# Two more chunks of an attention are turned by strided copies and VectorE, in a kernel that feeds a mixture of experts

## The chip, the cores and the metric

The kernel runs on one core of a Trainium2 chip. The engines of that core are PE (TensorE, the matrix array, with its weight loads shown apart as PEld), DVE (VectorE), ACT (ScalarE), POOL (GpSimd) and SP (SyncE, which here does nothing but issue transfers); 16 DMA engines move the data. Each engine works through its own queue in order, and semaphores tie the queues together. The metric is the device time of one execution in microseconds (us); a kernel's time is the median over its runs.

## The reference

Everything is float32. A lightning attention with a decay per head runs over 4 batches, 8 heads, 768 positions and 64 columns a head, in blocks of 64 positions. Its output, turned to 3072 rows of 512, goes through four experts (512 to 1024 to 512) whose results are added with normalised weights.

```python
for b in range(nb):                       # blocks of 64 positions
    intra = (qb @ kb^T * Dmask) @ vb      # Dmask: lam ** distance, lower triangle
    inter = (qb * lam_pow) @ kv_state
    out[:, :, sl] = intra + inter
    kv_state = lam_block * kv_state + (kb * rev_pow)^T @ vb
x = out.transpose(0, 2, 1, 3).reshape(3072, 512)
for e in range(4):
    h = maximum(x @ w1[e], 0)
    y += p[:, e:e + 1] * (h @ w2[e])      # p: domain_probs, each row divided by its sum
```

## The kernel before

**Tiling.** The 3072 rows are 24 chunks of 128 positions (n = 0 to 23: two blocks of one batch, all heads), in three groups g of eight. `where(n)` gives a chunk's place along the sequence and its batch: chunks 8 to 11 are the third and fourth 128 positions of batches 0 and 1, chunk 12 the third of batch 2. The expert products of a group with an expert are a unit; there are twelve, and each runs as fast-multiplication products M1 to M7 (seven products in place of eight, on sums and differences of blocks, and the same again inside each), in the order M1, M5, M6, M2, M7, M3, M4 (`SEQ`).

**The main loop.** For each unit (`at`) and each of its seven products (`i`) there are eight steps (`x`), numbered (at·7 + i)·8 + x through the whole kernel. In the stretch that matters here a step is eight matmuls of PE, by turns of the second product of one unit (`second_product`, L1233, x even) and of the first product of the next unit (`first_product`, L1174, x odd); at x = 5 there are four. So unit number 2 of the first products runs while `at` is 1 (steps 56 to 111), and unit 3 while `at` is 2 (from 112). Step 73 is the first that multiplies by M6's weight operand of unit 2, step 129 that of unit 3. Each step also takes a job or two from lists for VectorE (`lately`, `background`, `own_sums`), feeds a weight operand (`feed`), lets the attention work due at this step go, issues a small copy (`trickle`) at some steps, and pumps the planner.

**Weight operands.** The operands of the first products are sums of blocks of w1. GpSimd makes them (`prepare_w1`): in a row M1, the sum S1, M5, S3, M7, S2 (with a load of a block), M6, M2, S4, M3, M4. Each M is four subtractions into a stage tile `ops`, which is stored to a scratch tensor in DRAM (`w_ops` in the profile); each S is two additions or subtractions into a stage tile `w1o`. `feed` on SP reads an operand back from DRAM into two tiles `ws_in`, part a (384 KB) and part b (512 KB), nine or so steps before PE reads them. The stage tiles are a ring of seven buffers, shared by the loaded blocks (`w1b`), `w1o`, `ops` and the tiles `to` below, so a new one waits until the tile that had its buffer is stored.

These jobs are called chores. The planner that puts them in the queues while the program is built keeps estimates of what each engine has been given. In `pump` (L208) a chore begins only if GpSimd is free by its estimate and the transfers asked for (`asked`, `moved`) are less than `FULL` = 4 steps ahead. If `feed` needs an operand that has not been made, `until` (L232) forces chores to begin there and then.

**The attention.** A group's chunks run among the products of the group before. For each chunk a run stands at a step of the hand-written list `AT` (chunk 8 at 34, 9 at 40, and so on): `both` first finishes the chunk before (`values`, L824 and L842, tiles `op`), then starts its own (`scores`, L761 and L768, tiles `sp`). The chunk's q and k must be turned first, so that the columns of the heads lie on the partitions. There are two ways. Through PE: `turn` (L714) makes eight transposes (L727, into the banks `qp` and `kp`) and two copies on ACT (L735, L736), four steps before the run. Or across, from chunk `FIRST_ACROSS` on: pieces of q and k are copied from DRAM to DRAM (tile `across`) so that each 32 columns of a head stand as rows of 128 bytes (`bring_across`, `trickle`); `load_across` loads the chunk as `qx` and `kx`, 12 steps before the run, and VectorE turns their blocks of 32 by 32 (`turn_across`, L707), seven steps before it. The pieces of a batch are issued in the order of `rank`; `load_more` first issues all pieces that its batch still needs. A piece holds all the positions of the batch from the first chunk that comes across.

The output of two chunks is gathered in two tiles `xc`. Then `pair_sums` (L874), a chore too, stores them to `x_blocks`, makes four differences on GpSimd (tile `to`), and stores these.

Of the kernel before, what the change touches and what calls it, by code (L numbers as in the profile page):

```python
# [21 lines left out]
def kernel(  # L22
# [40 lines left out]
    CPG = 8  # L63
# [4 lines left out]
    W = 512  # L68
# [54 lines left out]
    def vector(n, psum):  # L123
        filled[0] = max(filled[0], now[0] + psum / 2) + 0.09 + n * (0.31 if psum else 0.8 if spare else 0.49) / 512
# [357 lines left out]

    FIRST_ACROSS = CPG + 4
    across = dram.tile([2, P, NHP, B, 16, 32], FP32, name="across")
    pieces = []
    rank = {0: 0, 2: 1, 3: 2, 1: 3}

    def bring_across(b):  # L490
        c = min(where(n)[0] for n in range(FIRST_ACROSS, NG * CPG) if where(n)[1] == b)
        for x, of in enumerate((q, k)):
# [8 lines left out]
    def trickle(m=1, by=None):  # L501
        for _ in range(m):
            if pieces:
                pieces.pop(0)[1](by)

    def comes_across(n):
        return n >= FIRST_ACROSS

# [133 lines left out]
    background = []  # L642
# [15 lines left out]
    def fits():  # L658
        return filled[0] - now[0] < 0.6
# [42 lines left out]
    def turn_across(n):  # L702

        qT, kT = nat.pop((n, "qx")), nat.pop((n, "kx"))

        def across(x):
            nc.vector.transpose(out=x[:], in_=x[:])  # L707
            vector(W, False)
            if x is kT:
                turned[n] = qT, kT, qT  # L710

        soon(n, *(lambda x=x: across(x) for x in (qT, kT)))
# [172 lines left out]
        ))  # L885

    FILL = {1: 18, 2: 43}
    AT = (34, 40, 47, 53, 58, 91, 99, 108, 115, 147, 154, 167, 172, 203, 210, 223)
    V_AHEAD = {CPG + 10: 8, CPG + 13: 10}
    steps = []  # L890

    def attention():

        first, last = CPG, NG * CPG - 1
        for n in range(first, last + 1):
            s = AT[n - first]
            turns_at = s - (7 if comes_across(n) else 4)
# [952 lines left out]
    for at, (g, e) in enumerate(units):  # L1850
        if at == 0:
            chores.extend(prepare_w2(2) + prepare_w1(3) + prepare_w2(3))
            chores.extend(prepare_w2_ops(2, False) + prepare_w1(0))
            for x in (3, 0):
                chores.extend(prepare_w2_ops(x, True))
        ahead = units[at + 1] if at + 1 < len(units) else None
        nested, nests = at >= NEST, ahead and at + 1 >= NEST
        if at == NEST:
            until(("w1", 0, "M4"))
            chores.extend(prepare_w2_ops(1, True))  # L1860
            spare.append(True)
        if at == NEST - 1:
            packed.append(True)
        blocks, banks = {}, {}
        for i in range(7):
            if fill2:
                feed2(*fill2.pop(0))
            if not nested:
                later_operands(g, e, SEQ2[i])
            if nested or (nests and i == 6):  # L1870
                for _ in range(4 if not nested else 2 if ahead else 16 if i == 0 else 4 if i > 1 else 0):
                    if fill3:
                        feed3(*fill3.pop(0))
            if nests and i == 2:
                nc.scalar.dma_start(
                    out=gate_bc, in_=gate_rows[ahead[0] - 1, :, ahead[1]].partition_broadcast(P),
                )
            if nested:
                pair = (at * 7 + i) % 2 if ahead else i % 3
                idle[:] = [(("q11", "q12"), ("q01", "q02"))[pair % 2], False]  # L1880
                b = nested_product(at, SEQ3[i], (("q01", "q02"), ("q11", "q12"), ("g1", "g3"))[pair])
                if i < 6 and (at, SEQ3[i + 1]) != PLAIN:
                    inner_sums(at, SEQ3[i + 1])
            else:
                b = second_product(g, e, SEQ2[i], banks)
            if nests and i == 6:
                inner_sums(at + 1, SEQ3[0], nested)
                if at + 1 == EARLY[0]:
                    inner_sums(*EARLY, True)
            a = []  # L1890
            if ahead:
                a = first_product(*ahead, SEQ[i], blocks, ("g1", "g3"))
            if nested and (at, SEQ3[i]) == END:
                b[6:6] = [lambda: (give("M4", 1, ("s0", "s1"), (1,)), turn_end(1, "q11"))]
                b[5:5] = [lambda: (give("M4", 0, ("s0", "s1"), (1,)), turn_end(0, "q12"))]
            if not ahead:
                order = [[], b[0:2], [], b[2:4], [], b[4:6], [], b[6:]]
            elif nested:
                order = [b[0:2], a[0:2], b[2:4], a[2:4], b[4:5], a[4:6], b[5:8], a[6:]]
            else:  # L1900
                order = [b[0:1], a[0:2], b[1:2], a[2:4], b[2:3], a[4:6], b[3:5], a[6:]]
            turned_back = list(after_last.get(SEQ3[i], ())) if nested and not ahead else []
            if at == i == 0:
                for m in SEQ[1:]:
                    own_x_apart(m, g, 0)
            resting[0] = at == NEST - 1 and i >= 5 or at == NEST and i == 0 or at == NEST - 2 and i == 5
            for x, part in enumerate(order):
                for f in part:
                    if f:
                        f()  # L1910
                now[0] += 1
                put = False
                if at == 0:
                    idle[:] = [("s0", "s1"), i < 3]
                    put = put_back()
                    take(own_sums)
                if nested and ahead:
                    idle[1] = x in ((1, 4) if i < 5 or at > NEST + 1 else (4,)) and (at - 2 * E + 1, i, x) not in held_at
                    put = put_back()
                added = first_steps.pop((at - 2 * E + 1, i, x), None)  # L1920
                if added:
                    added()
                all_added(now[0])
                if joins and not background:
                    joined()
                elif added and x > 2 or put:
                    pass
                elif (ahead or x % 2 == 0 and x + i) and not (nests and i == 6 and x == 7):
                    if nested or nests:
                        if lately:  # L1930
                            take(lately)
                        else:
                            rest()
                        if at == 2 * E and i in (2, 3) and fits():
                            rest()
                    else:
                        took = False
                        for of in (lately, background, own_sums):
                            if of and (not took or fits() or of is background and len(of) > 4):
                                take(of)  # L1940
                                if of is lately and i == 0:
                                    take(of)
                                took = True
                if nested or nests:
                    take(aside)
                    if own_sums and (nested or fits()):
                        take(own_sums)
                if ending and fits():
                    end_first()
                if nested and ahead and x in (1, 3) and fill3:  # L1950
                    feed3(*fill3.pop(0))
                if turned_back and x > 0:
                    for y in turned_back.pop(0):
                        if SEQ3[i] == END[1]:
                            give(*y[:2], ("s0", "s1"), *y[2:])
                        else:
                            give_across(*y)
                if fill and at * 7 + i >= 6 and x in ((0, 1) if at * 7 + i < 13 else (1, 3, 5) if at * 7 + i == 13 else FEED[nested]):
                    feed(*fill.pop(0))
                while steps and (at * 7 + i) * 8 + x == steps[0][0]:  # L1960
                    steps.pop(0)[1]()
                if at == 0 or x % 2 or at == 1 and x == 4:
                    trickle(1, nc.scalar if x % 2 else None)
                for h in range(1, NG):
                    if x == 3 and 0 <= at * 7 + i - FILL[h] < 7:
                        x_fill(h, SEQ[at * 7 + i - FILL[h]])
                pump(PACE[g])
# [30 lines left out]
```

## Time and profile before

| | |
|---|---|
| median of three runs | 1141.27 us (1141.19 to 1144.36) |
| profiled execution | 1142.07 us, its span 1140.3 us |
| PE busy | 99% of the span |
| DVE, POOL, ACT busy | 67%, 67%, 33% |
| transfers | 267.12 MB in 326,828 packets, 153,216 of them under 512 B |
| chunk copies `across` | 128 pieces, on the queues of SP and of ACT |
| loads of `qx`, `kx` from `across` | 12 each, 256 KB, 4.8 us to landing (median) |

The profile is of one execution, whose own time is 1142.07 us; the span, from the first to the last recorded instruction, is 1.8 us shorter. Times of PE, DVE, ACT and POOL are busy times; a queue such as SPq shows issuing, and a transfer lands some microseconds after its issue. A row of the timeline gives start, duration, engine, line, operation, tiles and count; in brackets stand the idle time before it and what ended it. Nearly all operations of DVE and POOL are issued by a helper at L117 and nearly all transfers by one at L114, so the tiles tell them apart.

### The profile page before, as it was taken

What the parts mean: (1) busy time and instruction counts of PE and PEld (TensorE: products, weight loads), DVE (VectorE), ACT (ScalarE), POOL (GpSimd) and SP (SyncE); (2) the same over time, 40 slices, a digit from 0 to 9 for tenths busy, and PEclk for the clock granted to TensorE, in tenths of its full rate; (3) what the DMA queues carried; (4) which work ended last, traced back from release to release, by engine and by line L of the source; (5) the groups of instructions that cost most, each with busy time, mean ns of one, the idle gap of its engine ahead of it and who ended that gap; (6) DMA issues with size and microseconds to landing.
All of it is one profiled execution on the core that took longest, in us unless ns stands there. A gap on an engine that the chain in (4) does not pass through costs nothing.

```text
span 1140.3 us, 22080 instructions
## 1 busy us (share of the span) xinstructions
PE 1130.5 (99%) x7983; PEld 988.2 (87%) x7983; DVE 769.0 (67%) x1474; ACT 380.3 (33%) x768; POOL 761.0 (67%) x730
## 2 busy tenths in 40 slices
PE   8999999999999999999999999999999999999998
PEld 7888888888888888888888888888888888888887
DVE  4576776587577658737655566878767576776785
ACT  3325123212312321232343442444354452342332
POOL 2838147644843786447687997994996873873885
PEclk9999999999999999999999999999999999999999
DMA  9795889999899989769557858886577757657552
GB/s 204 180 287 166 212 222 279 291 270 335 262 292 320 316 291 282 222 222 314 177 177 261 283 180 281 290 272 204 180 264 244 218 162 207 194 160 211 171 194 74
DMA packets 326828, 267.12 MB, mean 234 GB/s; under 512 B 153216, under 2 KB 270144, under 8 KB 326720
## 3 DMA queue, kind: packets, MB, share of 16 engines
q1 hardware_dynamic: 289472, 258.14, 73.1%
q10 hardware_dynamic: 37216, 7.57, 3.5%
q8 instruction: 64, 1.05, 0.4%
q14 instruction: 44, 0.36, 0.1%
q0 software_dynamic: 32, 0.00, 0.0%
HBM read 197.97 MB, written 73.96 MB: 238 GB/s over the span
## 4 chain that ended last, share of the span: by engine, by line
PE 98%; DVE 1%; issue 0%; DMA 0%; ACT 0%; DVEq 0%; POOLq 0%; ACTq 0%
PE pg L1174 41%; PE pq L1550 25%; PE q L1233 21%; PE pM L1692 2%; PE pc L1692 2%; PE op L824 1%; PE sp L761 1%; PE op L842 1%; PE sp L768 1%; PE pM L1417 1%; PE pg L1550 1%; PE qp L727 1%; PE kp L727 0%; DMA decay<-in_lam_dram 0%; PE yp L1377 0%
## 5 line engine op out<-in xcount | busy, mean ns | idle before, releaser
L1174 PE MATMUL pg<-xs,ws_in 128*128 128x256 f32 x1960 | 470.1, 380 | 0.0
L1174 PEld LDWEIGHTS pg<-xs,ws_in 128*128 128x128 f32 x1960 | 371.1, 190 | 52.8 <-DVE m L117 2.4
L117 DVE TENSOR_TENSOR m<-pg,m 128x512 f32<-128x512 f32 x374 | 255.4, 685 | 92.4 <-PE pg L1174 82.5
L1233 PE MATMUL q<-w2t,m 128*128 128x256 f32 x1120 | 265.6, 380 | 0.0
L1233 PEld LDWEIGHTS q<-w2t,m 128*128 128x128 f32 x1120 | 211.7, 190 | 29.3 <-issue 0.3
L117 DVE TENSOR_TENSOR sums<-pq,sums 128x256 f32<-128x256 f32 x272 | 112.9, 420 | 90.6 <-PE pq L1550 76.9
L1550 PE MATMUL pq<-acc,w2t 128*128 128x256 f32 x688 | 169.2, 379 | 0.0
L117 POOL TENSOR_TENSOR m<-m,decay 128x512 f32<-128x512 f32 x91 | 114.5, 1270 | 78.7 <-ACT m L1191 52.1
L1550 PEld LDWEIGHTS pq<-acc,w2t 128*128 128x128 f32 x688 | 130.6, 190 | 17.9
L1191 ACT ACTIVATE m<-m 128x512 f32<-128x512 f32 x99 | 62.4, 630 | 192.5 <-DVE m L117 190.6
L1251 DVE SCALAR_TENSOR_TENSOR acc<-q,gate,acc 128x256 f32<-128x256 f32 x108 | 52.0, 482 | 79.1 <-PE q L1233 78.6
L117 DVE TENSOR_TENSOR m<-m,m 128x512 f32<-128x512 f32 x108 | 92.9, 861 | 6.5 <-ACT m L1157 6.5
L1187 ACT COPY m<-pg 128x512 f32<-128x512 f32 x88 | 51.5, 585 | 122.0 <-PE pg L1174 108.7
L1151 ACT COPY pg<-m 128x512 f32<-128x512 f32 x77 | 45.4, 590 | 113.0 <-DVE m L117 103.3
L117 POOL TENSOR_TENSOR acc<-hT,hT 128x512 f32<-128x512 f32 x56 | 70.3, 1272 | 15.0 <-PE pq L1550 9.9
L117 POOL TENSOR_TENSOR acc<-hT,acc 128x512 f32<-128x512 f32 x56 | 71.2, 1272 | 6.4 <-PE pq L1550 2.7
L1550 PE MATMUL pq<-hT,w2t 128*128 128x256 f32 x288 | 70.0, 379 | 0.0
L117 POOL TENSOR_TENSOR w2o<-w2b 128x512 f32<-128x512 f32 x26 | 33.9, 1325 | 45.8 <-DMA w2b<-in_moe_w_dram 39.3
L1550 PEld LDWEIGHTS pq<-hT,w2t 128*128 128x128 f32 x288 | 54.7, 190 | 7.4
L1155 ACT COPY m<-pg 128x512 f32<-128x512 f32 x44 | 25.7, 585 | 89.6 <-PE pg L1174 84.8
L1550 PE MATMUL pq<-m,w2t 128*128 128x256 f32 x228 | 55.4, 379 | 0.0
L1005 ACT COPY hp<-m 128x512 f32<-128x512 f32 x84 | 48.5, 589 | 15.6 <-DVE hT L117 14.1
(157 smaller groups left out, 1419.5 us busy)
## 6 DMA issues: line engine op xcount, KB each, us to landing
ws_in<-w_ops SPq DMA_DIRECT2D x40, 512.0 KB, 5.1
w2t<-w_ops SPq DMA_DIRECT2D x72, 256.0 KB, 3.2
ws_in<-w_ops SPq DMA_DIRECT2D x60, 256.0 KB, 3.5
ws_in<-w_ops SPq DMA_DIRECT2D x40, 384.0 KB, 4.0
w2b<-in_moe_w_dram SPq DMA_DIRECT2D x56, 256.0 KB, 5.0
w_ops<-ops SPq DMA_DIRECT2D x28, 512.0 KB, 5.5
w_ops<-ops SPq DMA_DIRECT2D x54, 256.0 KB, 4.3
w2t<-w_ops SPq DMA_DIRECT2D x100, 128.0 KB, 2.8
```

Source lines behind the costliest of these rows:

```text
L117: eng.tensor_tensor(out=o, in0=a, in1=b, op=op)
L727: nc.tensor.transpose(out=x[:, ac * C:(ac + 1) * C], in_=y[:, ac].rearrange("p r d -> p (r d)"), identity=ident[:],)
L1005: nc.scalar.copy(out=there[x][:], in_=blk[at][:])
L1151: nc.scalar.copy(out=banks[tags[1]][:], in_=new["11"][:])
L1155: nc.scalar.copy(out=o[:], in_=p[:])
L1174: nc.tensor.matmul(out=p[:, j * 256:(j + 1) * 256], lhsT=ws[i][:, j * P:(j + 1) * P], rhs=xs[i], start=(fresh and j == 0), stop=True, skip ...
L1187: nc.scalar.copy(out=new[at][:], in_=p[:])
L1191: nc.scalar.activation(out=new[at][:], in_=new[at][:], func=AF.Relu)
L1233: nc.tensor.matmul(out=p[:, s * DH:(s + 1) * DH], lhsT=h[A_OF[m]][:, c * 256 + s * P:c * 256 + (s + 1) * P], rhs=fed2[g, e, m][uu][:, c], ...
L1251: nc.vector.scalar_tensor_tensor(out=o, in0=x, scalar=w, in1=o, op0=ALU.mult, op1=ALU.add)
L1550: nc.tensor.matmul(out=p[:, 0:256], lhsT=fed3[e, m, i][:, c * P:(c + 1) * P], rhs=b[B_OF[i]][:, c * 256:(c + 1) * 256], start=(fresh and c ...
L1692: nc.tensor.matmul(out=p[:, s * 256:(s + 1) * 256], lhsT=a[c][:, f:f + P], rhs=b[:, c, j * 256:(j + 1) * 256], start=(s == 0 and c == 0 an ...
```

## The change

Chunks 10 and 11 are turned across instead of through PE (`FIRST_ACROSS`), the order of batches in the copies follows (`rank`), and the planner books the VectorE transposes as it books operations on PSUM (`vector(W, True)`, an estimate of their length and no instruction). Four runs of the attention move: chunk 10 from step 47 to 48, 11 from 53 to 54, 12 from 58 to 60, 14 from 99 to 100, and with each its loads, turn and decay. In the first unit a second job is taken from the VectorE list when more than two wait, not four. And SP issues one more piece at odd steps of the first unit and at x = 0 and 6 of the next three products.

```diff
-    FIRST_ACROSS = CPG + 4
+    FIRST_ACROSS = CPG + 2
...
-    rank = {0: 0, 2: 1, 3: 2, 1: 3}
+    rank = {0: 0, 1: 1, 2: 2, 3: 3}
...
             nc.vector.transpose(out=x[:], in_=x[:])
-            vector(W, False)
+            vector(W, True)
...
-    AT = (34, 40, 47, 53, 58, 91, 99, 108, 115, 147, 154, 167, 172, 203, 210, 223)
+    AT = (34, 40, 48, 54, 60, 91, 100, 108, 115, 147, 154, 167, 172, 203, 210, 223)
...
-                            if of and (not took or fits() or of is background and len(of) > 4):
+                            if of and (not took or fits() or of is background and len(of) > (2 if at == 0 else 4)):
...
                 if at == 0 or x % 2 or at == 1 and x == 4:
                     trickle(1, nc.scalar if x % 2 else None)
+                if x % 2 and at == 0 or at == 1 and i < 3 and x in (0, 6):
+                    trickle()
```

PE has 4038 instructions in its program instead of 4054 (16 transposes less), DVE four more, ACT 32 fewer (four copies, 28 pieces), SP 26 more; POOL has the same ones in another order. The number of pieces stays 128, and those of batches 0 and 1 hold 12 rows of 32 positions instead of 8.

## The prediction

> **What bounds the kernel now.** I read the page's busy times and chain first, then the matmuls in order of time, then POOL's and SP's queues in the stretch that the change touches, then the transfers.
>
> ```profile
> span 1140.3 us, 22080 instructions
> PE 1130.5 (99%) x7983; PEld 988.2 (87%) x7983; DVE 769.0 (67%) x1474; ACT 380.3 (33%) x768; POOL 761.0 (67%) x730
> PE 98%; DVE 1%; issue 0%; DMA 0%; ACT 0%; DVEq 0%; POOLq 0%; ACTq 0%
> ```
>
> PE is busy 99% of the span and is 98% of the chain, so a gain can only be PE work removed plus the few holes PE has: 1140.3 − 1130.5 = 9.8 us, most of it in the load at the start and the stores at the end. A loss is any operand that comes later than PE wants it. In the stretch of the change the timeline of PE reads:
>
> ```profile
> 213.68 0.81 PE L1174 MATMUL pg<-xs,ws_in 128*128 128x256 f32 x3
> 214.33 1.89 PE L1233 MATMUL q<-w2t,m 128*128 128x256 f32 x8
> 216.06 1.89 PE L1174 MATMUL pg<-xs,ws_in 128*128 128x256 f32 x8
> 217.78 1.89 PE L1233 MATMUL q<-w2t,m 128*128 128x256 f32 x8
> 219.51 1.89 PE L1174 MATMUL pg<-xs,ws_in 128*128 128x256 f32 x8
> ```
>
> A step is 1.73 us; the short row is always step x=5 of a product, so the rows are steps 69 to 73, and 219.51 is step 73: the first matmuls that read the weight operand M6 of the third unit (unit number 2). How that operand comes to be, on POOL and on SP:
>
> ```profile
> 191.40 1.42 POOL L117 TENSOR_TENSOR ops<-w1o 128x256 f32<-128x256 f32 x2
> ...
> 197.33 0.72 POOL L117 TENSOR_TENSOR to<-xc 128x256 f32<-128x256 f32 x1 [2.25 <-ACT xc L863]
> ...
> 204.16 2.50 POOL L117 TENSOR_TENSOR w1o<-w1o,w1b 128x512 f32<-128x512 f32 x2 [3.92 <-DMA w_ops<-ops]
> 206.73 1.41 POOL L117 TENSOR_TENSOR ops<-w1o 128x256 f32<-128x256 f32 x2
> ```
>
> ```profile
> 198.01 1.46 SPq L114 DMA_DIRECT2D w_ops<-ops  x1
> ...
> 209.77 0.34 SPq L114 DMA_DIRECT2D w_ops<-ops  x1
> 210.16 1.26 SPq L114 DMA_DIRECT2D w_ops<-w1o  x2
> 212.90 1.11 SPq L114 DMA_DIRECT2D ws_in<-w_ops  x2
> ```
>
> M7's sums (191.40) are stored at 198.01; the sum S2 (204.16) waits for that store, 6.15 us after its issue, because its stage buffer is M7's. M6's sums follow (206.73 to 209.75), are stored at 209.77, and SP reads them back at 212.90, 3.1 us later. A ws_in of 384 KB lands 4.0 us after issue (median): about 216.9, against a need at 219.51. **So 2.6 us of slack** is all that M6 has, though M7 was summed a whole product earlier.
>
> **What the change removes.** Chunks 10 and 11 lose their TensorE turns:
>
> ```profile
> L727 PE MATMUL qp<-ident,qn x48: 272/273/473, 4.4 to 176.9; 128*128 128x128 f32 x48
> ...
> L735 ACT COPY qT<-qp x12: 567/586/632, 5.5 to 177.3; 128x512 f32<-128x512 f32 x12
> ```
>
> Transposes overlap in the array: in the matmul timeline one group of 4 takes 0.44 us (150.14 to 150.58), so a chunk's 8 take 0.87 and two chunks **1.74 us**, all on the bounding engine. The four ACT copies (4 × 0.59) are off the path (ACT 33% busy): 0. Moving runs later also removes some small PE holes (0.15 at 182.8, 0.19 near step 59, 0.1 at 201.95): −0.3, bounds 0 and −0.7.
>
> **What it adds off the path.** Four VectorE transposes of qx/kx, 0.70 us each: 2.8 us of DVE, which is 61 to 77% busy in the windows between 150 and 195. They are turned seven steps (12 us) ahead of the run that reads them, so 0; with that cover gone, 0.7 a transpose. SP issues 26 more DMAs at some 0.56 us: 14.6 us of SP time between 0 and 200. ACT issues 28 fewer. The copies for batches 0 and 1 grow from 8 to 12 rows of 32 columns: 32 KB to 48 KB, 64 pieces × 128 = 8192 more packets of 128 B. The second hardware queue, which between 140 and 240 us carries only such copies, prices them:
>
> ```profile
> q10 hardware_dynamic: 13216, 1.64, 10.6%
> ```
>
> 0.106 × 100 us × 16 engines / 13216 = 12.8 ns a packet; 8192 of them are 6.6 us of all 16 engines, spread over the first 230 us, with DMA already 86 to 96% busy in the windows from 150 to 240. No PE instruction reads them directly: 0 in the sum, up to +4 in the range (second rival).
>
> [...]
>
> **What it moves, and what that costs.** AT puts the runs of chunks 10, 11, 12 and 14 at steps 48, 54, 60, 100 instead of 47, 53, 58, 99. The planner begins a weight sum only if its count of transfers asked for is less than four steps ahead; the larger copies keep that count high, so the sums begin later, and several begin only when SP's feed demands them. In the built order of instructions M7, S2, M6 and M2 of unit 2 all stand on POOL at step 64 behind the four pair sums of chunks 10 and 11 (before: M7 at 56, pair sums at 58, S2 at 61, M6 at 63). The buffers follow: S2 takes the one of `to`, M6's sums take M7's, so **M6's sums wait for M7's store to land**, and SP's read of M6 waits for M6's own store. In times of this trace:
> - PE: by step 64 before (204.84) all runs are over; less 2.0 that is 202.8, and step 73 comes at 217.5.
> - The run of step 60 then lies at about 196 to 198; the pair (xc) was ready 0.6 us behind its run before, and its last additions now stand in step 61: 199.5 (198.8 to 200.5).
> - Pair sums 4 × 0.72 = 2.9: 202.4. M7's sums 3.0 (206.73 to 209.75 is such a set): 205.4. Store landing 6.0 (w_ops<-ops median 5.5, here 6.15): 211.5; S2's 2.5 us fit in meanwhile. M6's sums 3.0: 214.5. Store to read-back 4.0 (between the rows' 3.1 above and 4.9 at unit 3): 218.6. Issue and landing 4.4: 223.0.
> - Stall of PE 223.0 − 217.5 = **5.5 us**. By the shortest landings shown (2.7, 2.7, 2.3) it ends at 215.6: 0. With the longest (store 7.3, read-back 4.9, landing 5, xc at 200.5) about +10. The median of landings is the nearest row.
>
> The same shape comes once more in unit 3: M7, S2 and M6 all stand at step 117 behind the pair sums, before only M6 did (M7 at 111, S2 at 113):
>
> ```profile
> 300.46 0.73 POOL L117 TENSOR_TENSOR to<-xc 128x256 f32<-128x256 f32 x1 [2.63 <-DVE xc L117]
> ...
> 303.32 1.42 POOL L117 TENSOR_TENSOR ops<-w1o 128x256 f32<-128x256 f32 x2
> ```
>
> There M6 was read back at 311.61, and step 129 needs it at 320.66: 5 us of slack. Now, relative to PE: pair sums from 300.8 to 303.7, M7 to 307.1, its store 313.1, M6 316.1, read-back 320.1, landed 324.3: **3.6 us** (0 to 6).
>
> **Sum**, on the profiled execution (1142.07; span 1140.3 and 1.8 around it): 1142.07 − 1.74 − 0.3 + 5.5 + 3.6 = 1149.1. The median of the runs shown is 0.8 lower: **1148.3 us**.
>
> **Rivals.**
> 1. *The removed turns stand alone.* Place: M6 of units 2 and 3. For it: POOL is 67% busy and each store may land in 2.7 us; the point is M6 landing by 217.5, that is 18 us after xc. Against: four dependent pieces that sum to 23 by medians. Time: 1141.27 − 2.0 = 1139.2, so not slower, and no change within the measurement.
> 2. *Transfers or VectorE become the bound too.* More 128 B packets at a DMA 90% busy delay qx/kx of chunk 12 (loaded at step 48 behind the last of batch 2's copies, turned at 53 to 55, landing 3.3 to 7.8) and the landings above by up to 6.6 us, less 2.6 of slack: 4 more. [...] For it: SP waited 19.9 us in all for these copies. Against: by step 79 they are done, before only at 136, so later stretches get lighter. Time with both chains: 1152.3, at the long ends 1157.
> 3. *Only the first chain stalls*, unit 3 keeping its slack since the copies have ended by then: 1139.2 + 5.5 = 1144.7 or a little over.
>
> **How the numbers follow.** Forecast 0.56 (own range 1145 to 1153); rival 1, 0.16; rival 2, 0.12; rival 3, 0.16. A difference under 0.3% (3.4 us) can't be told from none: faster means below 1137.9, which rival 1 reaches only if some unseen wait goes too, 0.03; slower is over 1144.7, all of rival 2, nearly all of the forecast and half and more of rival 3, 0.79; the rest, 0.18, is within. The range is 1140.5 to 1157: rival 1 is its low side, the long landings its high side.
>
> **What would show it.** PE L727 qp/kp at 40 each, not 48, and DVE transposes of qx and kx at 14. Right: a PE hole of 3 to 9 us ahead of the L1174 matmuls near 218, a second of 1 to 6 near 327 (320.66 plus what was lost), both with POOL waiting on w_ops<-ops ahead of the M6 sums and SP's ws_in behind their store. Wrong: PE without holes over 1 us there, or M7's sums on POOL well before the pair sums; or holes ahead of the attention's matmuls (L761, L824) instead, which is rival 2.

## The result, and the profile after

| | before | after |
|---|---|---|
| median of six runs | 1142.68 us | 1170.15 us (1168.24 to 1171.83) |
| ratio, with its 95% interval | | 1.0239 (1.0224 to 1.0254) |
| span of the profiled execution | 1140.3 us | 1166.4 us |
| PE busy in it | 1130.5 us | 1138.6 us |

The change makes the kernel 2.4% slower, some 27 us where 7 were forecast. The page of the kernel after, its span and the first line of the busy times:

```profile
span 1166.4 us, 22041 instructions
PE 1138.6 (98%) x7967; PEld 990.9 (85%) x7967; DVE 769.9 (66%) x1478; ACT 378.3 (32%) x764; POOL 766.0 (66%) x730
PE 90%; DMA 5%; POOL 2%; DVE 1%; issue 1%; SPq 0%; ACT 0%; POOLq 0%; DVEq 0%; ACTq 0%
```

The last of these lines is the chain that ended last, by engine: PE had 98% of it and has 90% now, and transfers and POOL's sums stand on it instead. PE has 16 matmul records fewer (7967 for 7983), as it should, and yet is busy 8 us longer. What PE waited for, in all of the kernel after (total, times, longest):

```profile
PE pg L1174 <- DMA ws_in<-w_ops: 9.0, 3, 5.2
PE pg L1174 <- POOL ops L117: 3.1, 1, 3.1
PE sp L768 <- issue: 2.9, 3, 1.2
PE pg L1174 <- DVE m L117: 2.8, 2, 2.3
PE op L824 <- DVE qx L117: 1.5, 1, 1.5
```

In place, in PE's timeline of the kernel after:

```profile
105.39 1.13 PE L1174 MATMUL pg<-xs,ops 128*128 128x256 f32 x4 [3.11 <-POOL ops L117]
...
198.92 3.49 PE L1174 MATMUL pg<-xs,ws_in 128*128 128x256 f32 x8 [2.30 <-DVE m L117]
...
220.49 3.75 PE L1174 MATMUL pg<-xs,ws_in 128*128 128x256 f32 x8 [2.97 <-DMA ws_in<-w_ops]
...
241.89 3.75 PE L1174 MATMUL pg<-xs,ws_in 128*128 128x256 f32 x8 [5.22 <-DMA ws_in<-w_ops]
```

These are steps 9, 57, 65 and 73; the first hole lies in the middle of step 9 and holds up step 10, and is called the hole at step 10 here and in the expectations (which put it at 3.4 us). A step's eight matmuls take 1.89 us as a rule, and 3.5 to 3.75 behind the last three holes: the granted clock is 0.50 there. The stretches of the kernel after by windows (length, busy times of the engines, clock, share of the DMA engines, GB/s):

```profile
105.00:115.00 10.00, 9.61 (x45) 8.47 (x46) 4.34 (x9) 2.77 (x5) 9.69 (x12) 1.00 0.84 248
...
220.00:226.00 6.00, 5.51 (x13) 4.46 (x14) 0.00 (x0) 1.17 (x2) 0.00 (x0) 0.50 0.90 279
...
241.00:247.00 6.00, 5.11 (x12) 4.15 (x13) 2.01 (x3) 0.00 (x0) 5.69 (x9) 0.50 0.95 284
```

Set against the kernel before, step by step, the matmuls of the kernel after begin 0.5 us earlier at step 0, 2.9 later at step 10, 2.3 later at step 47, 7.8 at step 57, 15.8 at step 66, 22.4 at step 73 and 25.0 at step 75. From there to the end the distance hardly changes (26.0 at the last step), so nearly all of the loss lies in the first 250 us. From step 73 to step 75 nothing was waited for: these 2.6 us are the half clock behind the last hole.

**Where it comes from.** SP's queue ahead of the hole at step 10, in the kernel before and then in the kernel after:

```profile
83.09 2.86 SPq L114 DMA_DIRECT2D across<-in_k_dram  x4
87.01 1.60 SPq L114 DMA_DIRECT2D w2b<-in_moe_w_dram  x2
```

```profile
85.27 10.83 SPq L114 DMA_DIRECT2D across<-in_k_dram  x6
96.14 1.28 SPq L114 DMA_DIRECT2D across<-in_q_dram  x2
99.33 0.89 SPq L114 DMA_DIRECT2D w2b<-in_moe_w_dram  x2
```

Before, SP issued four copies here in 2.86 us and then those two loads of `w2b` at 87.01; now there are eight copies, and the loads come 12 us later. One of the copies was held 5.7 us and the first load 1.9, each until a copy on ACT's queue had landed (issued at 93.35 and 96.80). Nothing that these transfers read or write orders them. In the built program each transfer of SP and ACT adds to one of eight completion counters, in turn, and is held until the transfer that used its counter last, the eighth before it, has landed. The trace of the change shows it: its 1188 transfers of SP and ACT land on eight counters, and of the 1180 that had one before them on their counter none was issued until that one had landed (the copy at 95.55 behind a landing at 95.53, the load at 99.33 behind one at 99.31). SP is thus also held by what ACT issues late. An extra copy costs SP its issue of 0.6 us, and a turn at the counters.

The lateness of SP then goes three ways. POOL, in the kernel after:

```profile
167.86 1.06 POOL L117 TENSOR_TENSOR kn<-kn,decay 128x512 f32<-128x512 f32 x1 [11.21 <-DMA kn<-in_k_dram]
...
183.03 1.06 POOL L117 TENSOR_TENSOR kn<-kn,decay 128x512 f32<-128x512 f32 x1 [10.21 <-DMA kn<-in_k_dram]
...
229.19 2.50 POOL L117 TENSOR_TENSOR w1o<-w1o,w1b 128x512 f32<-128x512 f32 x2 [9.44 <-DMA x_blocks<-to]
```

POOL stands for ten microseconds at a time before kn (50.1 us in all, 8.1 in the kernel before), which SP has loaded late, and the weight sums stand behind it; S2, the last row, waits 9.4 us for a store that SP issues late. VectorE stands before qx (7.11 us ahead of the transpose at 197.58), with sums behind it that PE's banks wait for: that is the hole at step 57. And SP's own read-backs of weight operands come late: the holes of steps 65 and 73.

### The profile page after: what moved, and what is told of

It is laid out like the page before. It is cut to its first block, busy times and chain, and to the rows that moved or that the text cites. A ratio compares the mean times of both kernels' runs of the same rounds, so it can differ in the third digit from the quotient of the medians.

```text
span 1166.4 us, 22041 instructions
## 1 busy us (share of the span) xinstructions
PE 1138.6 (98%) x7967; PEld 990.9 (85%) x7967; DVE 769.9 (66%) x1478; ACT 378.3 (32%) x764; POOL 766.0 (66%) x730
## 4 chain that ended last, share of the span: by engine, by line
PE 90%; DMA 5%; POOL 2%; DVE 1%; issue 1%; SPq 0%; ACT 0%; POOLq 0%; DVEq 0%; ACTq 0%
PE pg L1174 38%; PE pq L1550 24%; PE q L1233 18%; PE pM L1692 2%; PE pc L1692 2%; POOL ops L117 1%; PE op L824 1%; DMA ws_in<-w_ops 1%; DMA w_ops<-w1o 1%; PE sp L761 1%; PE op L842 1%; PE sp L768 1%; DMA w_ops<-ops 1%; POOL to L117 1%; PE pM L1417 1%
## 5 line engine op out<-in xcount | busy, mean ns | idle before, releaser
L1174 PE MATMUL pg<-xs,ws_in 128*128 128x256 f32 x1960 | 475.9, 383 | 12.3 <-DMA ws_in<-w_ops 9.0
L1233 PEld LDWEIGHTS q<-w2t,m 128*128 128x128 f32 x1120 | 214.1, 192 | 30.6 <-issue 0.6
L117 DVE TENSOR_TENSOR m<-m,m 128x512 f32<-128x512 f32 x108 | 90.1, 834 | 5.9 <-ACT m L1157 5.9
L117 POOL TENSOR_TENSOR kn<-kn,decay 128x512 f32<-128x512 f32 x16 | 17.8, 1112 | 98.8 <-DMA kn<-in_k_dram 50.1
```

What stands on the lines that cost most here:

```text
L117: eng.tensor_tensor(out=o, in0=a, in1=b, op=op)
L1174: nc.tensor.matmul(out=p[:, j * 256:(j + 1) * 256], lhsT=ws[i][:, j * P:(j + 1) * P], rhs=xs[i], start=(fresh and j == 0), stop=True, skip ...
L1233: nc.tensor.matmul(out=p[:, s * DH:(s + 1) * DH], lhsT=h[A_OF[m]][:, c * 256 + s * P:c * 256 + (s + 1) * P], rhs=fed2[g, e, m][uu][:, c], ...
```

## The experiments

Each is compared with the kernel before, run on the same chip; the kernel before itself lay between 1142.1 and 1146.2 us (medians of the sets), so the ratios are read. 0.001 is 1.1 us.

| run | what | ratio (95%) |
|---|---|---|
| the change | | 1.0239 (1.0224 to 1.0254) |
| e1 | change, extra copies on ACT | 1.0115 (1.0079 to 1.0151) |
| e2 | change, sums early | 1.0227 (1.0199 to 1.0254) |
| e3 | before, with the extra copies | 1.0110 (1.0088 to 1.0133) |
| e4 | change, without the extra copies | 1.0312 (1.0294 to 1.0331) |
| e5 | e1 and e2 together | 1.0066 (1.0049 to 1.0083) |
| e6 | before, with larger copies | 1.0031 (1.0010 to 1.0053) |
| e7 | change, filler matmuls | 1.0244 (1.0213 to 1.0275) |
| e8 | change, kn loaded first | 1.0235 (1.0201 to 1.0268) |
| e9 | change, eight stage buffers | 1.0294 (1.0225 to 1.0362) |
| e10 | before, eight stage buffers | 1.0043 (1.0016 to 1.0069) |
| e11 | e5 with eight stage buffers | 1.0032 (1.0007 to 1.0056) |
| e12 | change, old AT | 1.0192 (1.0140 to 1.0244) |
| e13 | before, with 34 tiny transfers on SP | 1.0090 (1.0056 to 1.0124) |
| e14 | before, extra copies on ACT | 0.9990 (0.9965 to 1.0016) |
| e15 | e11, those of the second unit on SP | 1.0093 (1.0058 to 1.0129) |
| e16 | e11, extra copies in the first unit alone | 1.0101 (1.0080 to 1.0121) |
| e17 | e16 with seven stage buffers | 1.0126 (1.0105 to 1.0146) |

### Which part makes the loss: e1 to e4

**e1.** The queue of the extra copies.

```diff
                 if x % 2 and at == 0 or at == 1 and i < 3 and x in (0, 6):
-                    trickle()
+                    trickle(1, nc.scalar)
```

> The changed kernel with the extra copies issued on ACT's queue instead of SP's; bytes, packets and the order of POOL's sums are the same. If SP's queue being late is the cause (26 more issues at some 0.56 us, each of which also waits for the transfer eight before it), the hole at step 10 (3.4 us at 104.3) goes, the waits of POOL for kn (11.2, 10.2, 10.9 us) shrink below 5 us each, and the time falls to 1143 to 1155. If the late order of M7, S2 and M6 is the cause by itself, the hole before step 73 stays at 4 to 6 us and the time is over 1160. If the larger copies load the DMA engines too much, wherever they are issued, the time stays at 1165 to 1175.

Half the loss goes (1.0239 to 1.0115, some 14 us). The waits of POOL for kn fell only partly: there is still one of 12.2 us, and the holes at steps 10 (2.4 us) and 73 (4.7) stay. So SP's queue is a cause, and not the only one.

**e2.** The order of the sums, which the prediction held for the cause.

```diff
-    FULL = 4
+    FULL = 8
```

> The changed kernel with FULL = 8 instead of 4, so that POOL's weight sums begin as early as in the kernel before (one forced job for M6 of unit 2, none of M7 and S2); copies and AT as in the change. If the order of the sums is the cause: no hole over 1 us before steps 73 and 129 and a time of 1139 to 1150. If SP is late by its own load: the hole at step 10 stays (3.4), POOL still waits 10 us each time for kn, and the time is 1158 to 1170.

Nothing gained: 1.0227, within the interval of the change. POOL still waits 52.7 us in all for kn (50.1 in the change), and with S2's and M7's sums standing early in its queue PE still has holes of 3.5 us at step 65 and 3.9 at step 73. The hole at step 10 has grown from 3.1 to 5.5 us, so what the order gained at step 73 may be lost there. To mend the order alone doesn't take the loss away.

**e3.** The extra copies alone.

```diff
                     trickle(1, nc.scalar if x % 2 else None)
+                if x % 2 and at == 0 or at == 1 and i < 3 and x in (0, 6):
+                    trickle()
```

> The kernel before with only the extra copies on SP added (chunks 10 and 11 still turned by PE, the same bytes in all as before, AT as before, nearly no sum forced). If SP's queue is the cause: the hole at step 10 is there (2 to 4 us), kn, qn and qx arrive later, and the time is 1146 to 1160. If the late sums or the larger copies are the cause, no hole at step 10 and 1140 to 1144.

The two lines alone, on the kernel before, cost 12.6 us: as the SP theory had it, with the hole at step 10 (2.4 us, which e13 will show to be of another cause) and, which it had not said, one of 4.9 us at step 73.

**e4.** The change without them.

```diff
-                if x % 2 and at == 0 or at == 1 and i < 3 and x in (0, 6):
-                    trickle()
```

> The changed kernel without the extra copies on SP. If SP's early load alone makes the loss, the hole at step 10 goes; but 33 of the copies are then left for the step before chunk 12 is loaded (57 left at step 48, 24 at 56) and go out in one burst on SP. By the SP theory that burst blocks SP for 33 x 0.56 = 18 us or more, the loads of chunk 12 and the first weight operands (steps 57 to 73) come later than in the changed kernel, and the time is no better: 1160 to 1185. By the theory of the late sums alone: 1145 to 1155.

1.0312, worse than the change. On SP 25 of the left-over copies went out in one burst of 17.6 us ahead of chunk 12's loads, fewer than the 33 that were expected, and PE has a hole of 10.1 us that ends at 199.6:

```profile
180.67 5.98 SPq L114 DMA_DIRECT2D across<-in_q_dram  x9
186.70 11.57 SPq L114 DMA_DIRECT2D across<-in_k_dram  x16
198.31 0.63 SPq L114 DMA_DIRECT2D qx<-across  x1
```

The hole at step 10 did not go (2.4 us). The extra copies are needed once chunks 10 and 11 come across: against this run they win 8 us on SP (1.0239) and 22 on ACT (1.0115).

### Number or bytes: e6, e13 and e14

**e6.** The larger copies alone.

```diff
-        c = min(where(n)[0] for n in range(FIRST_ACROSS, NG * CPG) if where(n)[1] == b)
+        c = min(where(n)[0] for n in range(CPG + 2, NG * CPG) if where(n)[1] == b)
```

> The kernel before with the copies of batches 0 and 1 as large as in the change (12 rows of 32 positions, 1 MB and 8192 packets of 128 bytes more), which nothing reads; as many copies as before, at the same steps, and chunks 10 and 11 by PE. If the bytes matter by themselves (6.6 us of all DMA engines): 1147 to 1156, with SP's waits for earlier copies longer and a hole at step 10. If only the number of copies on SP matters: 1141 to 1146 and no hole at step 10.

1.0031: the larger copies cost 3.5 us (1.1 to 6.1), between the two expectations, with holes of 2.4 us at step 10 and 2.9 at step 89 (the first that reads M7). At step 10 POOL waited 8.4 us for a buffer that PE was still reading, not for a transfer, so the 8192 packets by themselves cost less than 3.5 us; how much less is not shown.

**e13.** The number alone.

```diff
+    unread_rows = dram.tile([34, 8, 64], FP32, name="unread")
+    unread = [unread_rows[y] for y in range(34)]
...
+                if x % 2 and at == 0 or at == 1 and i < 3 and x in (0, 6):
+                    y = unread.pop(0)
+                    nc.sync.dma_start(out=y, in_=q[0, 0, 0:8, :])
```

> The kernel before with a transfer of 2 KB from DRAM to DRAM, which nothing reads, on SP at each of the 34 places where the change issues an extra copy; the real copies stay where they were. If the number of issues on SP and their turns at the completion counters make the loss: most of e3's 12 us, 1151 to 1157, with the hole at step 10. If it is the copies' bytes, moved earlier into a loaded stretch: 1141 to 1146 and no hole.

34 transfers of 2 KB that nobody reads cost 10 us (1.0090), most of what the copies of e3 cost. Each held SP 0.63 us (median), as a copy of 48 KB does (0.61 to 0.62 in the change). Of the two signs that were named, the hole at step 10 did not come, so that hole has another cause; the hole at step 73 did:

```profile
PE pg L1176 <- DMA ws_in<-w_ops: 6.6, 2, 5.0
```

(PE's waits of e13; its line 1176 is line 1174 of the kernel before.) Its POOL queue holds M7's sums ahead of the pair sums, as in the kernel before:

```profile
191.17 1.41 POOL L117 TENSOR_TENSOR ops<-w1o 128x256 f32<-128x256 f32 x2
...
197.08 0.72 POOL L117 TENSOR_TENSOR to<-xc 128x256 f32<-128x256 f32 x1 [2.23 <-DVE xc L117]
...
211.78 2.50 POOL L117 TENSOR_TENSOR w1o<-w1o,w1b 128x512 f32<-128x512 f32 x2 [11.80 <-DMA w_ops<-ops]
```

```profile
205.25 1.34 SPq L114 DMA_DIRECT2D w_ops<-ops  x1
```

M7 was summed from 191.2 to 194.8, but SP issued its store only at 205.25 (198.01 in the kernel before), and S2 waited 11.8 us where it had waited 3.9.

**e14.** The bytes without SP: the diff of e3, with `trickle(1, nc.scalar)`.

> The kernel before with the extra copies on ACT's queue instead of SP's (e3 had them on SP and lost 12 us). If the bytes in the loaded stretch make the loss, whoever issues them: 1152 to 1159. If SP's queue makes it: 1142 to 1149.

0.9990 (0.9965 to 1.0016): no loss that can be told. The program of e14 differs from that of e3 in the queue of these copies and what the build derives from it. The turns at the counters are as many in both, so it is SP's own time that costs, not the turns alone. Its POOL queue has M7 behind the pair sums, the very order that the prediction feared:

```profile
203.19 0.72 POOL L117 TENSOR_TENSOR to<-xc 128x256 f32<-128x256 f32 x1 [7.68 <-DVE xc L117]
...
206.04 2.39 POOL L117 TENSOR_TENSOR ops<-w1o 128x256 f32<-128x256 f32 x2
...
211.07 2.49 POOL L117 TENSOR_TENSOR w1o<-w1o,w1b 128x512 f32<-128x512 f32 x2 [1.03 <-DMA x_blocks<-to]
```

S2 waits 1.03 us for the store of `to`, where in e3, with the same order, it waited 7.99; and PE has no hole of over 0.7 us between step 1 and the end. With SP in time, that order is harmless in the kernel before.

### Links and other causes: e7 to e10, e12

**e7.** The half clock. Ahead of the first matmul of the operand:

```diff
+    FILLED = {(2, "M1"): 8, (2, "M5"): 10, (2, "M6"): 18}
...
+            if i == "M1" and (unit_of[g, e], m) in FILLED:
+                for _ in range(FILLED[unit_of[g, e], m]):
+                    nc.tensor.matmul(
+                        out=p[:, 0:256], lhsT=ident[:], rhs=xs[i], start=True, stop=True, skip_group_check=True,
+                    )
```

> The changed kernel with matmuls of the identity, whose results are overwritten, ahead of the first matmul of steps 57 (8), 65 (10) and 73 (18): PE works inside the three holes (2.5, 3.1, 5.4 us) instead of idling. If the half clock seen behind these holes comes from the idle time, the granted clock stays 1.0 there and the time falls by 5 to 8 us, to 1162 to 1165, though PE has 36 matmuls (7.8 us) more. If it does not, the time is 1168 to 1174.

The fillers were mis-sized: 10 and 18 of them stand in the trace as 20 and 36 records and took 4.3 and 7.9 us, longer than two of the holes, and at step 57 PE waited for a bank and not for the operand, so that those did not fill it. The clock stayed up all the same (e7 by windows, then its last filler and step 73):

```profile
220.00:226.00 6.00, 6.00 (x30) 5.28 (x29) 0.48 (x1) 0.90 (x2) 2.94 (x5) 1.00 0.95 243
...
241.00:247.00 6.00, 5.78 (x27) 4.79 (x26) 0.00 (x0) 0.00 (x0) 5.84 (x8) 1.00 0.54 141
```

```profile
237.97 7.93 PE L1176 MATMUL pg<-xs,ident 128*128 128x256 f32 x36
246.12 1.99 PE L1180 MATMUL pg<-xs,ws_in 128*128 128x256 f32 x8 [0.22 <-DMA ws_in<-w_ops]
```

With the holes at steps 65 and 73 filled there is no half clock behind them, and none at step 57 either (1.00 from 195 to 205), where 2.1 us stayed idle; but no time was won (1.0244). Step 73 still had to wait 0.22 us behind 7.9 us of filler. What the half clock costs in the change is not settled by this run. The 2.6 us behind step 73 reach the end; behind steps 57 and 65 the slower matmuls cover part of the next wait for an operand, and what is left of them is not shown.

**e8.** Is kn the link from SP to the sums? `load(n, "k")` one step earlier and ahead of the copies and of qx and kx:

```diff
             load_across(n)
-            load(n, "k")
...
+            if comes_across(n):
+                steps.append((turns_at - 6, lambda n=n: load(n, "k")))
```

> The changed kernel with the load of kn (for the chunks that come across) issued one step earlier and ahead of the flush of copies and the loads of qx and kx. If POOL's wait for kn (11.2, 10.2, 10.9 us) is the link from SP's lateness to the weight sums, those waits shrink to below 6 us, the holes of steps 57 to 73 shrink by 3 to 6 us together and the time falls to 1158 to 1167. If kn is only another victim, the time stays at 1168 to 1172.

1.0235, no gain; POOL still waits 39.0 us for kn. kn is one victim of SP among others.

**e9 and e10.** Are seven stage buffers too few?

```diff
-    stage = ctx.enter_context(tc.tile_pool(name="stage", bufs=7))
+    stage = ctx.enter_context(tc.tile_pool(name="stage", bufs=8))
...
-NPOOL = 42
+NPOOL = 40
```

> The changed kernel with eight stage buffers instead of seven (and 40 instead of 42 small tiles, to make room). If the stores' landings decide because a sum takes the buffer of a tile stored shortly before (S2 that of `to`, M6 that of M7), the POOL waits of 9.4 us ahead of S2 and of 5.8 us ahead of the sums of step 7 go, the holes at steps 10 and 73 fall below 1.5 us, and the time is 1150 to 1160. If SP's queue and the read-backs set the pace anyway, the holes only move and the time stays at 1165 to 1173.

> The kernel before with eight stage buffers and 40 small tiles, the control of e9. Its sums hardly wait for buffers on PE's path, so 1140 to 1146; if two small tiles fewer make waits of their own, 1146 to 1155, and e9 has to be read against that.

1.0294 for the change and 1.0043 for the kernel before: an eighth buffer doesn't help while SP is late (6.6 us is the longest wait for an operand), and two small tiles fewer make waits of their own.

**e12.** The change with `AT = (34, 40, 47, 53, 58, 91, 99, ...)`.

> The changed kernel with AT as before (47, 53, 58, 99): runs, loads and turns of chunks 10, 11, 12 and 14 one or two steps earlier. If the later places were what made room, the lateness of SP meets the runs sooner and the time rises to 1172 to 1185. If the moved runs add to the loss: 1160 to 1168.

1.0192: by this ratio some 1165 us, which is in the second range, but the interval overlaps that of the change. Whether the moved runs add to the loss is open; they are not most of it.

### Repairs put together: e5, e11, e15 to e17

**e5** has the diffs of e1 and e2, **e11** those and the eight stage buffers, **e15** is e11 with the extra copies of the second unit on SP again, **e16** is e11 without those, and **e17** is e16 with seven buffers and 42 small tiles. The expectations stand in this order.

> The changed kernel with the extra copies on ACT's queue (as e1) and FULL = 8 (as e2). e2 alone gained nothing, e1 alone 12 us. If SP's lateness hides what the earlier sums could give, the two together give more than e1: the hole before step 73 (4.8 us in e1) falls below 2 us and the time to 1143 to 1151. If the sums' order never mattered, as in e1: 1153 to 1158.

> The changed kernel with the three repairs together: extra copies on ACT, FULL = 8, eight stage buffers (40 small tiles). If SP's load, the sums' order and the ring are the whole loss, what is left is the gain of the removed turns, and the time is 1139 to 1144, no slower than before. If the larger copies or ACT's queue cost something too: 1145 to 1152.

> e11 (copies on ACT, FULL = 8, eight stage buffers) with the extra copies of the second unit, at x = 0 and 6, on SP again, since e11 has a hole of 2.7 us at 194 where PE waits for ACT, whose queue has waited for its copies. If those copies on ACT make that hole, it goes and the time is 1143 to 1148; if they then make SP late as in the change, 1150 to 1160.

> e11 with the extra copies in the first unit alone (on ACT), none in the second: six copies fewer before step 78. If they made ACT late at 194, that hole (2.7 us) goes and the time comes to 1141 to 1146; if SP gets the rest in one burst ahead of chunk 13's load instead and that hurts, 1147 to 1153.

> e16 with seven stage buffers and 42 small tiles as in the change. The hole of 2.4 us at step 10 is back (POOL's sums wait for a buffer that PE reads until step 7), and small waits of the pool of small tiles go: 1143 to 1149, at most 4 us from e16.

e5 comes to 1.0066: the early sums, worth nothing in e2, are worth 5.6 us once the extra copies have left SP (1.0115 to 1.0066, intervals apart), and the hole at step 73 falls from 4.7 to 1.1 us. So in the change the order of the sums is a part of the loss. e11 comes to 1.0032, e10's price of two small tiles included; its largest hole, 2.7 us, is PE waiting for ACT, which had waited for copies. Against the expectation, that hole stays in e15, at 196 (3.7 us), where six or so copies on SP cost 7 us, and without the copies of the second unit e16 and e17 are 8 and 11 us worse than e11, slower than was expected of either. The hole at step 10 is back in e17 (2.4 us), as expected. No version with chunks 10 and 11 across was faster than the kernel before; e11 comes nearest.

## Why the prediction was wrong

The direction was right, and of the two holes that it named one came in its size, 5.2 us ahead of step 73; the other, ahead of step 129, was under 1 us. The size of the loss was a quarter of what came.

- **The removed turns**, 1.74 us: 8 of 48 transposes gone from each of qp and kp, as said, and PE 0.5 us earlier at step 0. The gain itself is buried in the rest.
- **The step that failed** is the one on SP: "SP issues 26 more DMAs at some 0.56 us: 14.6 us of SP time between 0 and 200", which entered the sum as nothing. It was right as a price of issue (0.63 in e13) and wrong as a price on the path; no reason was given why nothing on the path should wait for it. SP was not an idle engine in that stretch: its queue carries, in order, the loads and stores on which POOL, VectorE and PE wait. e13 prices the number of issues alone at 10 us (6 to 14), e3 the copies themselves at 12.6. Rival 2 came close to it when it read that SP waits 19.9 us for these copies; that row holds the copies of k alone, and those of q add 10.7. It priced their bytes, though, and not SP's queue.
- **The late sums**: 5.5 us were forecast at step 73 and 5.2 measured, but that the sizes agree is luck. The long wait was not that of M6's sums for M7's store: S2 waited 9.4 us for the store of `to`, which SP issued late, and M6's sums followed S2 at once. And the order of the sums is by itself neither needed for the hole nor enough for it: e13 keeps the order of the kernel before and has the same hole (5.0), e14 has the feared order and no hole. It takes part once the change is there: 5.6 us in e5, hidden in e2 as long as SP is late. The chain of store, landing and read-back was rightly seen, and the slack in it was eaten by SP. At step 129 a hole of 3.6 us was forecast, and 0.8 came.
- **The larger copies**, 0 in the sum with up to +4 in the range: 3.5 us (1.1 to 6.1) in e6, within its bounds, and in the profiled run 2.4 us of it by a stage buffer and not by packets.
- **Holes at other steps** (10, 57, 65) were not in the sum. At step 10 POOL's sums wait for a stage buffer that PE reads until step 7 (5.77 us in the change, 8.44 in e6); the built program gave that tile another buffer than before. The hole that this makes takes 2.4 us in e1, e3, e4, e5, e6 and e17, and is not there in e13 and e14. In the change it is 3.1 us, since SP's late load of `w2b` ends last there. Why the build gave another buffer was not traced.
- **Holes that add to themselves**: the half clock behind a hole (0.50, for 3.41 to 6.83 us) was not weighed. PE's busy time shows it, 8.1 us up though 1.7 of work is gone. Of this the 2.6 us behind step 73 reached the end; for the rest it stays open (e7).

In the trace of the change the granted clock is 0.50 for 3.41, 6.83 and 6.83 us at the holes of steps 57, 65 and 73, and 1.00 in the rest of the stretch from 95 to 248 us. The three begin at 199.25, 219.73 and 240.21, that is 20.48 us apart, six times 3.41. In the 3.41 us ahead of each of them PE was busy for 0.33, 0.35 and none of the time, so at the first two it was not idle throughout.

The length of a hole doesn't tell where it came: the 2.30 us at step 57 were followed by the half clock and the 3.11 us at step 10 were not. Counted back from 199.25 in steps of 3.41 us, the hole at step 10 lies in two of them (100.27 to 103.68 and 103.68 to 107.09), and PE was busy for 0.59 and 0.50 of these. What decides it in general is not shown by four holes of one trace.

Still open besides: what the half of the loss that e1 leaves consists of. e6 gives 3.5 us of the 13 that remain in e1 (2.4 of them at step 10), and e5 shows that some 5.6 hang on the sums' start; the rest was not taken apart.

## What to carry to other kernels

An engine that only issues transfers, as SP here, can be the bound without one busy row on the page: count its issues in the stretch, and ask of each thing that it carries by how much it may slip. Transfers that nothing waits for should not stand in the queue that everything waits for: the same copies cost 12.6 us on SP and nothing on ACT. And a chain that has no slack for one reason can break for another; a repair of one cause may show nothing until the other is gone (e2 against e5).

## What the runs showed of the hardware

- A transfer of 2 KB holds SP as long as one of 48 KB: 0.63 us, median of 34 (e13), against 0.61 to 0.62 in the change.
- 34 transfers on SP's queue that move 70 KB in all make a kernel of 1142 us slower by 0.9% (e13).
- In the change the granted clock was 0.50, for 3.41 to 6.83 us, at holes of PE of 2.30, 2.97 and 5.22 us, and 1.00 at one of 3.11. With filler matmuls in the holes of steps 65 and 73 it stayed at 1.00 (e7).
